# The first matmul of seven chunks as Strassen products, and the row sums of q as two columns of another matmul

## The chip, the cores and the metric

The kernel runs on one core of a Trainium2 chip. Such a core has five engines with instruction queues of their own: TensorE (PE in the profile; its weight loads are listed apart as PEld and overlap with its matmuls), VectorE (DVE), ScalarE (ACT), GpSimd (POOL) and SyncE (SP). Each works through its queue strictly in order, and an instruction that needs another engine's result waits at the head of its queue. SBUF is the on-chip memory that all engines use; PSUM is the small memory that TensorE writes its results to, here used as eight banks of 128 x 512 fp32 values. DMA transfers are issued on the queues of SP, POOL and ACT.

The metric is the time of one execution in device microseconds; smaller is better.

## The reference

Two layers follow each other. The first is a linear attention for 8 batches, 8 heads, 576 rows and a head size of 64; the second is a residual MLP behind a layer norm.

```python
q_s = exp(q) / sum over d;   k_s = exp(k) / sum over rows     # shifts left out
kv  = einsum('bhsd,bhse->bhde', k_s, v)
x   = einsum('bhsd,bhde->bhse', q_s, kv)  -> [8, 576, 512]     # heads side by side
xn  = (x - mean) / sqrt(var + 1e-6) * g_ln
out = x + relu(xn @ w_ch1) @ w_ch2                             # 512 -> 2048 -> 512
```

Inputs and output are fp32. The kernel multiplies in bf16 with fp32 sums.

## The kernel before

**Tiling.** A batch has 576 = 4 x 128 + 64 rows. Chunks `c` = 0 to 7 are the first 512 rows of one batch each, as `T` = 4 tiles of 128 rows; the ninth, `c = C9 = 8`, collects the last 64 rows of all eight batches, again 512 rows. Chunks are counted from 0 here, as in the code. Each chunk passes through attention, layer norm, a first matmul with `w1` (512 to 2048), ReLU, and a second with `w2` (2048 to 512).

**The two matmuls.** TensorE computes the hidden layer transposed: 16 row tiles `m` of 128 hidden units, each as four matmuls over `ko` (128 x 128 weights, up to 512 rows of the chunk as columns). `mm1` does a whole row tile, 512 columns wide; `mm1_part` does half, 256 columns, since the first row tiles start before all four `t` of the transposed input `xnT` have landed. In chunks 2 to 8 four row tiles run as halves and twelve whole. ScalarE applies the ReLU (L402 and L439) into `hT`. The second matmul is already in Strassen's form in chunks 1 to 8: `mm2_fast` runs seven products of 16 half-width matmuls (L521) into banks `a`, `b`, `c`, `e`; VectorE makes the sums of `hT` that they need (`sum_h`, L505), ScalarE and VectorE copy and add banks (L546, L619, L549), and VectorE finishes with a scale and the residual (L532), from where POOL's queue stores the result.

**Attention of the next chunk** runs beside the matmuls of the current one. k and v are loaded as fp32 on SP's queue (`load_batch`), q too; ScalarE takes `exp` of both and, from chunk 3 on, casts v to bf16 (`cast_v`, L157). `kv_mm` sums `exp(k)` times v on TensorE into a PSUM tile per two head pairs (`pkv`, one bank each; a column of ones in `vm` brings k's sums), and VectorE divides that into `kv_sb` as soon as the two head pairs of a tile are complete (`recip_z` at L243, two multiplications at L268). `eq_T` transposes `exp(q)` by DMA. `po_mm` then multiplies it with `kv_sb`, one bank `po` for each row tile. VectorE adds up q's rows beforehand (`reduce_q`, L199) and inverts the sums (L742); `x_fast` scales `po` with them into `x` (L338), takes the mean (L344), and writes `xn = (x - mean) * g` (L331). ScalarE sums the squares (L325), and a second DMA transpose (`xn_T`) makes `xnT` for the next chunk's first matmul.

**PSUM.** Pool `mm_ps` has six banks for everything about the two matmuls, pool `att_ps` has two tiles of one bank, which `pkv` and `po` share.

**Order.** The order in each queue is written out by hand. `mlp_steps(c)` lists TensorE's main steps with a weight each (1 for a matmul of 512 columns, 0.5 for 256), and `run` inserts the side work: a side function with position p is issued when the weights of the main steps before it have reached p. So a chunk of 64 + 56 = 120 units is the clock by which attention, sums, loads and transposes are placed. For chunks 2 to 6, `attn_fast` spreads `kv_mm` of the next chunk over positions 2 to 20 and the four groups of `po_mm` over 22 to 28, 36 to 43, 60 to 70 and 80 to 92.5; `second_side` does the like in chunk 1, `attn_rest` places the ninth chunk's attention into chunk 7.

Of the kernel before, what the change touches and what calls it, by code (L numbers as in the profile page):

```python
# [3 lines left out]

# [16 lines left out]
def kernel(  # L21
# [16 lines left out]
    nc = tc.nc  # L38
# [16 lines left out]
    CAST = (1, 2)  # L55
    T0 = 6
# [11 lines left out]
    att_ps = ctx.enter_context(tc.tile_pool(name="att_ps", bufs=2, space=PS))  # L68
    mm_ps = ctx.enter_context(tc.tile_pool(name="mm_ps", bufs=6, space=PS))

    ident = const.tile([P, P], BF16)
    eps_ln = const.tile([P, 1], FP32)
# [6 lines left out]
    g_bc = const.tile([P, DM], FP32)  # L79
# [3 lines left out]
    kv_sb = const.tile([P, B, NP, P], BF16)  # L83
# [18 lines left out]
    raws = {}  # L102

# [3 lines left out]
    def alloc_kv(b):  # L107
        raws[b][0], raws[b][1], raws[b][3], raws[b][4] = (
            raw.tile([P, H, T, D], FP32, tag="kt", name="kt", bufs=1),
            raw.tile([P, H, T, D], BF16 if b in CAST else FP32, tag="vt", name="vt", bufs=1),  # L110
# [50 lines left out]
    def prep_kvrem(b):  # L161
        par = b % 2
        nc.scalar.activation(ekr[:, par], raws[b][3], AF.Exp)
        for half in range(2):
            ps = slice(SR * half, SR * half + SR)
            nc.vector.tensor_copy(
# [4 lines left out]
    def new_eq(c):  # L171
        eqs[c] = (
            att.tile([P, T, H, D], BF16, tag="eq", name="eq"),
            sml.tile([P, T, H], FP32, tag="zq", name="zq"),
            sml.tile([P, T, H], FP32, tag="rq", name="rq"),
        )
        eqTs[c] = att.tile([P, T, NP, P], BF16, tag="eqT", name="eqT")
# [41 lines left out]
    def exp_k0(j):  # L219
        hs = slice(2 * j, 2 * j + 2)  # L220
        if j == 0:
            eks[0] = raw.tile([P, T0, H, D], BF16, tag="vt", name="ek0", bufs=1)
# [8 lines left out]
    def z0_mm(j):  # L231

        if j % 2 == 0:
            kvbox["z0", j // 2] = mm_ps.tile([P, 2, 256], FP32, tag="m", name="z0")
# [11 lines left out]
    def kv_mm(b, j, t):  # L246
        par = b % 2
        last = T if b else T0 - 1
        if j % 2 == 0 and t == 0:
            kvbox["p", j // 2] = att_ps.tile([P, 2, 256], FP32, tag="a", name="pkv")  # L250
# [12 lines left out]
        if j % 2 == 1 and t == last:  # L263
            js = slice(j - 1, j + 1)
            rzk = recip_z(pkv[:, :, P]) if b else kvbox["rz", j // 2]
            for half in range(2):
                ps = slice(64 * half, 64 * half + 64)
                nc.vector.tensor_mul(  # L268
                    kv_sb[ps, b, js, ps], pkv[ps, :, ps],
                    rzk[ps].to_broadcast([64, 2, D]),  # L270
                )

    def start_x(c):
# [3 lines left out]
            mlp.tile([P, T, DM], BF16, tag="xn", name="xn"),  # L277
# [6 lines left out]
    def po_mm(c, t, i):  # L284


        if c < B:
            if i == 0:
                pool, tag = (mm_ps, "m") if c == 0 and t >= 2 else (att_ps, "a")
                pobox["p"] = pobox[c, t] = pool.tile([P, DM], FP32, tag=tag, name="po")  # L290
            nc.tensor.matmul(  # L291
                pobox["p"][:, i * P : i * P + P], eqTs[c][:, t, i, :], kv_sb[:, c, i, :],
                start=True, stop=True,
            )
        else:
            if i % 2 == 0:
# [765 lines left out]
```

## Time and profile before

| | |
|---|---|
| median of 6 runs | 280.12 us (279.82 to 280.55) |
| the profiled execution's own time | 279.94 us |
| its span in the trace | 278.2 us (1.74 us lie around it) |
| PE busy | 272.0 us, 98% of the span, 2242 matmuls |
| DVE busy | 195.1 us, 70% |
| ACT busy | 181.8 us, 65% |
| granted TensorE clock | 0.999 of full speed |
| one chunk, c = 2 to 6 | 28.10 to 28.11 us from start to start |
| last chunk, c = 8 | 26.08 us |

How to read it: matmuls are pipelined, so a matmul of 256 columns is listed with 273 ns although the next one starts 109 ns later. For TensorE the distance between starts counts, and it is taken from a row of matmuls in the timeline. Times on VectorE and ScalarE are from start to end of one instruction; two that don't depend on each other may overlap by some 0.1 us.

### The profile page before, as it was taken

How to read it: one execution, taken by the hardware profiler on the slowest of the kernel's cores; microseconds unless marked ns; L12 is line 12 of the kernel's file. 1: busy time of each engine (PE TensorE's matmuls, PEld its weight loads, DVE VectorE, ACT ScalarE, POOL GpSimd, SP SyncE). 2: the span in 40 equal slices, each digit the busy share in tenths (PEclk: the TensorE clock that was granted, in tenths of full speed). 3: DMA queues.
4: the chain of work that ended last, by engine and by line, in shares of the span. 5: the costliest groups of instructions: out<-in, count | busy, mean ns of one | idle time of the engine just before them, and what ended most of it. 6: DMA issues, size and time to landing. Idle time of an engine off the chain costs nothing.

```text
span 278.2 us, 5663 instructions
## 1 busy us (share of the span) xinstructions
PE 272.0 (98%) x2242; PEld 201.5 (72%) x2245; DVE 195.1 (70%) x457; ACT 181.8 (65%) x346; POOL 36.8 (13%) x64
## 2 busy tenths in 40 slices
PE   8999999999999999999999999999999999999994
PEld 6788755766995699558955895599658855885683
DVE  4772648988996688658865886588657929962363
ACT  4578862797887785778577856786585477526500
POOL 3932124300030003000300030003000300030000
PEclk9999999999999999999999999999999999999999
DMA  7999999899969996994599469545914410241014
GB/s 197 247 206 209 336 215 334 196 251 320 170 168 370 281 129 174 326 219 79 146 338 230 81 161 303 107 75 133 209 39 78 138 52 1 40 128 61 2 38 113
DMA packets 68845, 48.01 MB, mean 173 GB/s; under 512 B 40402, under 2 KB 65490, under 8 KB 68819
## 3 DMA queue, kind: packets, MB, share of 16 engines
q1 hardware_dynamic: 57074, 27.66, 43.1%
q0 software_dynamic: 11152, 19.47, 27.9%
q10 hardware_dynamic: 592, 0.52, 0.6%
q8 instruction: 17, 0.28, 0.4%
q14 instruction: 10, 0.07, 0.1%
HBM read 36.70 MB, written 9.44 MB: 166 GB/s over the span
## 4 chain that ended last, share of the span: by engine, by line
PE 90%; DMA 5%; DVE 3%; POOL 1%; issue 0%; DVEq 0%
PE ph L414 29%; PE ba L521 20%; PE ph L429 15%; PE bb L521 5%; PE be L521 5%; PE bc L521 5%; PE pc L474 4%; DMA w_sb<-in_moe_w_ch_dram 3%; PE pkv L259 3%; PE po L291 2%; DMA qt<-in_q_dram 2%; DVE x L338 1%; DVE xn L331 1%; PE ptr L803 1%; PE po L298 1%; POOL v L866 1%
## 5 line engine op out<-in xcount | busy, mean ns | idle before, releaser
L414 PE MATMUL ph<-xnT,w_sb 128*128 128x512 bf16 x368 | 87.2, 379 | 0.0
L402 ACT ACTIVATE hT<-ph 128x512 bf16<-128x512 f32 x92 | 53.5, 598 | 18.4 <-PE ph L414 18.3
L414 PEld LDWEIGHTS <-w_sb 128*128 128x128 bf16 x368 | 34.1, 98 | 34.5 <-issue 0.2
L521 PEld LDWEIGHTS <-hs 128*128 128x128 bf16 x512 | 49.2, 98 | 5.8 <-DVE hs L505 0.2
L429 PE MATMUL ph<-xnT,w_sb 128*128 128x256 bf16 (+1 forms) x432 | 52.7, 269 | 0.3 <-DMA w_sb<-in_moe_w_ch_dram 0.3
L439 ACT ACTIVATE hT<-ph 128x512 bf16<-128x512 f32 x48 | 28.6, 599 | 24.5 <-PE ph L429 24.3
L505 DVE TENSOR_TENSOR hs<-hT 128x1024 bf16<-128x1024 bf16 x32 | 21.9, 687 | 27.8 <-ACT hT L402 27.6
L429 PEld LDWEIGHTS <-w_sb 128*128 128x128 bf16 x432 | 38.4, 98 | 4.2 <-DMA w_sb<-in_moe_w_ch_dram 0.5
L521 PEld LDWEIGHTS <-hT 128*128 128x128 bf16 x384 | 36.6, 98 | 5.2 <-ACT hT L402 0.2
L538 POOL DMA_DIRECT2D out_dram<-ot x28 | 15.0, 541 | 179.7 <-DVE ot L532 155.9
L521 PE MATMUL ba<-w_q,hs 128*128 128x256 bf16 x256 | 31.3, 273 | 0.0
L331 DVE SCALAR_TENSOR_TENSOR xn<-x,mv,g_bc 128x512 bf16<-128x512 bf16 x34 | 25.6, 752 | 1.2
L338 DVE SCALAR_TENSOR_TENSOR x<-po,rq 128x512 bf16<-128x512 f32 x30 | 20.6, 687 | 6.5 <-PE po L291 6.1
L325 ACT ACTIVATE scrap<-x,mv 128x512 bf16<-128x512 bf16 x34 | 24.6, 723 | 0.1
L291 PE MATMUL po<-kv_sb,eqT 128*128 128x128 bf16 x128 | 24.1, 219 | 0.4 <-DVE x L338 0.2
L199 DVE TENSOR_REDUCE zq<-eq 128x8 f32<-128x512 bf16 x32 | 20.1, 687 | 4.2 <-ACT eq L191 2.5
L259 PE MATMUL pkv<-vm,ek 128*128 128x129 bf16 x112 | 21.2, 220 | 0.0
L546 ACT COPY s<-ba 128x512 f32<-128x512 f32 x15 | 8.8, 584 | 16.7 <-PE ba L521 16.7
L291 PEld LDWEIGHTS <-eqT 128*128 128x128 bf16 x128 | 11.7, 98 | 7.4 <-issue 0.6
L521 PE MATMUL ba<-w_sb,hT 128*128 128x256 bf16 x128 | 16.2, 273 | 0.0
L521 PE MATMUL bb<-w_q,hs 128*128 128x256 bf16 x128 | 15.8, 273 | 0.0
L521 PE MATMUL bc<-w_sb,hT 128*128 128x256 bf16 x128 | 15.7, 273 | 0.0
(117 smaller groups left out, 337.9 us busy)
## 6 DMA issues: line engine op xcount, KB each, us to landing
out_dram<-ot POOLq DMA_DIRECT2D x32, 256.0 KB, 3.0
qt<-in_q_dram SPq DMA_DIRECT2D x5, 1024.0 KB, 7.4
kt<-in_k_dram SPq DMA_DIRECT2D x5, 1024.0 KB, 7.1
vt<-in_v_dram SPq DMA_DIRECT2D x5, 1024.0 KB, 10.8
w_sb<-in_moe_w_ch_dram POOLq DMA_DIRECT2D x8, 512.0 KB, 13.2
qt<-in_q_dram POOLq DMA_DIRECT2D x2, 1024.0 KB, 15.8
kt<-in_k_dram POOLq DMA_DIRECT2D x2, 1024.0 KB, 16.0
kt<-in_k_dram SPq DMA_DIRECT2D x4, 288.0 KB, 5.7
```

Source lines behind the costliest of these rows:

```text
L199: nc.vector.reduce_sum(eqs[c][1][:, t], eqs[c][0][:, t], axis=AX.X)
L259: nc.tensor.matmul(pkv[:, j % 2, 0:w], lhsT, rhs, start=(t == 0 and j % 2 == 0), stop=(t == last), skip_group_check=True,)
L291: nc.tensor.matmul(pobox["p"][:, i * P : i * P + P], eqTs[c][:, t, i, :], kv_sb[:, c, i, :], start=True, stop=True,)
L325: nc.scalar.activation(scrap, x[:, t], AF.Square, bias=mv[:, t, 0:1], accum_out=mv[:, t, 1:2])
L331: nc.vector.scalar_tensor_tensor(xn[:, t], in0=x[:, t], scalar=mv[:, t, 0:1], in1=g_bc, op0=ALU.add, op1=ALU.mult)
L338: nc.vector.scalar_tensor_tensor(x[:, t].rearrange("p (h d) -> p h d", h=H), in0=pobox[c, t].rearrange("p (h d) -> p h d", h=H), scalar=1. ...
L402: nc.scalar.activation(dst, src, AF.Relu)
L414: nc.tensor.matmul(hbox["ph"], w1_sb[:, ko, m * P : (m + 1) * P], xnTs[c][:, :, ko, :], start=(ko == 0), stop=(ko == KO1 - 1),)
L429: nc.tensor.matmul(ph[:, m % 2, at : at + tn], w1_sb[:, ko, m * P : (m + 1) * P], xnTs[c][:, t0 : t0 + tn, ko, :], start=(ko == 0), stop=( ...
L439: nc.scalar.activation(dst, ph, AF.Relu)
L505: nc.vector.tensor_tensor(out=dst, in0=x, in1=y, op=op)
L521: nc.tensor.matmul(hbox[bank][:, t], lhsT, rhs, start=first and (own or t == 0) and k == 0, stop=k == KH - 1, skip_group_check=True)
```

## The change

It touches four things.

1. **First matmul.** In chunks 2 to 8, row tiles 4 to 15 become three groups of four. Each group is a 2 x 2 block product (two row tiles of hidden units against two, two `ko` against two, columns of `t` 0, 1 against 2, 3) done as seven products of four matmuls 256 columns wide (`prod1`) in place of eight. The sums of weight blocks are made once, in chunk 1 (`quarter_w1`); the differences of `xnT` blocks once per chunk on VectorE (`sums_x`). Per group ScalarE copies a bank (`seed`) and keeps two intermediate sums in SBUF (`keep_g`), VectorE adds two banks (`seed_b`) and finishes one quarter with an addition and a ReLU (`last_g`). Row tiles 0 and 1 stay halves, 2 and 3 whole. `plan["order"]` (`o9` in the ninth chunk) is the sequence of these tokens.
2. **q's sums.** `kv_sb` gets two more columns per head pair, with ones, so that `po_mm` delivers 130 columns and the sums of `exp(q)` stand in two of them. VectorE inverts them in `x_fast`; `reduce_q` goes for chunks 1 to 7. A `po` tile is now two banks, and so is the one `pkv` tile of all four head pairs; pool `att_ps` holds a single such tile, which both use in turn. `kv_sb` is written when all of `kv_mm` is done.
3. **g.** The weight `g_ln` is multiplied into `w1` once (`fold_w1`, in chunk 0, behind its first matmul), and `x_fast` writes `512 * x - sum` with one input tensor in place of `(x - mean) * g` with two; the factor 512 goes out again in `rstd_op`.
4. **v.** From chunk 3 on, v is loaded by eight DMAs on POOL's queue, one per head, that cast to bf16 straight into `vm`. The casts on ScalarE go; the two small copies of `prep_kvrem` move from VectorE to ScalarE.

All positions of side work are set anew (`plan`); a chunk is 58 + 56 = 114 units. The core of the diff:

```diff
+    plan = dict(
+        order=('part 0|P1 0|C 0|part 2|x 0|P5 0|P6 0|x 1|P1 1|C 1|P2 0|E 0|P7 0|P6 1|L 0|P2 1|P3 0|P5 1|P4 0|P1 2|C 2|P7 1|E 1|plain 2|L 1|P6 2|P3 1|P4 1|P5 2|E 2|P7 2|P2 2|plain 3|P4 2|L 2|P3 2').split('|'),
+        kv=[12.5, 26.0],
+        po=[[29.0, 36.0], [45.0, 47], [55.0, 66.0], [85.0, 88.0]],
...
+        rest=[[20, 31, 36, 43.5], [38.0, 38.5, 58.0, 65.5], [51.5, 58.0, 65.0, 74.0], [63.5, 80.5, 85.0, 87.0]],
...
+        kv2=[42.5, 47.5],
+        po2=[[56.5, 56.5], [61, 63], [78.0, 81.0], [89.5, 92.5]],
...
-    att_ps = ctx.enter_context(tc.tile_pool(name="att_ps", bufs=2, space=PS))
+    att_ps = ctx.enter_context(tc.tile_pool(name="att_ps", bufs=1, space=PS))
...
-        if j % 2 == 0 and t == 0:
-            kvbox["p", j // 2] = att_ps.tile([P, 2, 256], FP32, tag="a", name="pkv")
...
+        if b and j == 0 and t == 0:
+            whole = att_ps.tile([P, NP, 256], FP32, tag="a", name="pkv")
+            for half in range(2):
+                kvbox["p", half] = whole[:, 2 * half : 2 * half + 2]
...
-        if j % 2 == 1 and t == last:
...
+        if t == last and (j == NP - 1 or b == 0 and j % 2 == 1):
+            for jj in ((j // 2,) if b == 0 else range(2)):
+                pkv = kvbox["p", jj]
+                js = slice(2 * jj, 2 * jj + 2)
+                rzk = recip_z(pkv[:, :, P]) if b else kvbox["rz", jj]
+                for half in range(2):
+                    ps = slice(64 * half, 64 * half + 64)
+                    nc.vector.tensor_mul(
+                        kv_sb[ps, b, js, ps], pkv[ps, :, ps],
+                        rzk[ps].to_broadcast([64, 2, D]),
+                    )
...
+        elif c < B:
+            if i == 0:
+                pobox[c, t] = att_ps.tile([P, NP, 256], FP32, tag="a", name="po")
+            nc.tensor.matmul(
+                pobox[c, t][:, i, 0:VW], eqTs[c][:, t, i, :], kv_sb[:, c, i, :],
+                start=True, stop=True,
+            )
...
+            po = pobox[c, t]
+            nc.vector.reciprocal(rq, po[:, :, P:VW])
...
+        if c:
+            nc.vector.tensor_scalar(
+                out=xs[c][2][:, t], in0=x[:, t], scalar1=float(DM), scalar2=st[:, t, 0:1],
+                op0=ALU.mult, op1=ALU.subtract,
+            )
+            return
...
+    def fold_w1(ko):
+        nc.vector.tensor_scalar_mul(
+            out=w1_sb[:, ko, :], in0=w1_sb[:, ko, :], scalar1=g_col[:, ko : ko + 1]
+        )
...
+            dst, x, y = ((t1, b12, b11), (t2, b22, t1), (t3, b22, b12), (t4, b21, t2))[n]
+            nc.vector.tensor_sub(out=dst, in0=x, in1=y)
...
+        nc.tensor.matmul(hbox["q", slot][:, m], lhsT, rhs, start=first and i == 0,
+                         stop=ko == 1, skip_group_check=True)
...
+        def seed(g, src, dst):
+            hbox["q", dst] = bank_of([P, 2, 2 * P], FP32, "q", dst)
+            nc.scalar.copy(hbox["q", dst], hbox["q", src])
...
+        def seed_b(g):
+            a_, b_, c_, e_ = names(g)
+            hbox["q", e_] = bank_of([P, 2, 2 * P], FP32, "q")
+            nc.vector.tensor_tensor(out=hbox["q", e_], in0=hbox["q", b_], in1=hbox["s2", g], op=ALU.add)
...
+            nc.vector.tensor_tensor(out=dst, in0=hbox["q", b_], in1=hbox["s3", g], op=ALU.add)
+            nc.vector.tensor_scalar_max(dst, in0=dst, scalar1=0.0)
...
+            nc.scalar.copy(hbox[name, g], hbox["q", 10 * g])
...
-            nc.vector.memset(raws[b][which][0:1, 0, 0, 0:1], 0.0)
+            if which != 1:
+                nc.vector.memset(raws[b][which][0:1, 0, 0, 0:1], 0.0)
...
+            for h in range(H):
+                nc.gpsimd.dma_start(
+                    vm[:, b % 2, :, h // 2, 64 * (h % 2) : 64 * (h % 2) + 64],
+                    v[b, h, 0:SM, :].rearrange("(p t) d -> p t d", t=T),
+                )
```

## The prediction

> **What bounds the kernel now.** I read the page from the top: who is busy, then what the chain that ended last is made of, then single chunks. TensorE leads, and the chain is matmuls nearly throughout:
>
> ```profile
> PE 272.0 (98%) x2242; PEld 201.5 (72%) x2245; DVE 195.1 (70%) x457; ACT 181.8 (65%) x346; POOL 36.8 (13%) x64
> ...
> PE 90%; DMA 5%; DVE 3%; POOL 1%; issue 0%; DVEq 0%
> PE ph L414 29%; PE ba L521 20%; PE ph L429 15%; PE bb L521 5%; PE be L521 5%; PE bc L521 5%; PE pc L474 4%; DMA w_sb<-in_moe_w_ch_dram 3%; PE pkv L259 3%; PE po L291 2%; DMA qt<-in_q_dram 2%; DVE x L338 1%; DVE xn L331 1%; PE ptr L803 1%; PE po L298 1%; POOL v L866 1%
> ```
>
> 98% busy could still hide stalls, since pipelined matmuls count as busy. So I compare a chunk's length with its matmuls. The chain in order of time has 48 matmuls of 512 columns in 10.36 us (0.2158 us each) and 16 of 256 columns in 1.746 us (0.1091); the timeline has kv's start 0.057 us apart and po's 0.0555. A chunk of 2 to 6 has 144 of 256 columns, 48 of 512, 20 for kv and 16 for po: 15.71 + 10.36 + 1.14 + 0.89 = 28.10 us. The table by stage shows as much from start to start:
>
> ```profile
> core 0: us, PE busy (x) PEld busy (x) DVE busy (x) ACT busy (x) POOL busy (x), PEclk, DMA share, GB/s
> 107.65:135.76 28.11, 28.11 (x230) 20.83 (x229) 20.82 (x50) 20.28 (x38) 1.75 (x4) 1.00 0.81 198
> 220.08:248.12 28.04, 28.04 (x210) 20.20 (x209) 21.19 (x42) 16.88 (x37) 2.21 (x5) 1.00 0.21 58
> 248.12:274.20 26.08, 26.08 (x192) 18.55 (x190) 11.71 (x23) 10.14 (x17) 1.21 (x3) 1.00 0.19 61
> ```
>
> TensorE doesn't wait at all in these chunks. Every matmul taken out is a gain in full, and every wait put in costs in full. VectorE and ScalarE are busy 74% and 72% of such a chunk.
>
> **Matmuls: the gain.** Per chunk, 48 of 512 and 32 of 256 columns become 8 of 512, 16 halves and 84 products of 256: 13.85 us becomes 1.73 + 1.75 + 9.16 = 12.64. That is 1.21 us, in seven chunks 8.5 us. A weight load takes 98 ns (group L521) and is hidden behind 109 ns; the second matmul has run at this pace all along. The two extra columns of po cost 112 x 0.001 = 0.1 us. Net -8.4 us, if nothing waits.
>
> **Average load of the others.** VectorE loses four reductions (0.687 each), a reciprocal (0.353), four means (0.153) and two casts (0.284), 4.3 us; four xn go from 0.752 to about 0.29, 1.9 us. It gains four differences of 512 bf16 elements, three `seed_b` of 0.70 (row L549), three `last_g` of 0.69 + 0.29 and four reciprocals of 0.20 (row L816): 7.5 us. So +1.4: 22.2 of 26.9 us. Three prices have no row. A difference lies between a copy of 512 (0.288) and the two-input row of 1024 (0.687); I take 0.42, above half the latter. The one-input bf16 operations (xn, the ReLU in `last_g`, `fold_w1`) lie between that copy and 0.752; I take 0.29, as the copy has the same types, size and memory:
>
> ```profile
> L331 DVE SCALAR_TENSOR_TENSOR xn<-x,mv,g_bc 128x512 bf16<-128x512 bf16 x34 | 25.6, 752 | 1.2
> L505 DVE TENSOR_TENSOR hs<-hT 128x1024 bf16<-128x1024 bf16 x32 | 21.9, 687 | 27.8 <-ACT hT L402 27.6
> L159 DVE COPY vm<-vt 128x512 bf16<-128x512 bf16 x8 | 1.8, 288 | 3.7 <-DMA vt<-in_v_dram 3.7
> ```
>
> ScalarE loses three ReLUs (0.60) and four casts (0.61), and gains nine copies of a bank (0.57 to 0.58) and two small copies (about 0.4): +1.8, 22.1 of 26.9. Both engines fit on average, so what counts is who waits in which order.
>
> **The new wait: kv to po.** Before, `pkv` has two tiles and the first half is divided while the second is still being summed; po comes after it at leisure. After, all four multiplications stand behind the last kv matmul, and po needs the same single tile of `att_ps`, so the first po waits until the fourth has read it. The trace has this very sequence once, in chunk 0, where kv's end comes in one piece:
>
> ```profile
> 43.21 0.13 PE pkv L259 x2
> 43.34 0.02 issue
> 43.36 0.18 DVE rzk L243
> 43.57 0.28 DVE kv_sb L268
> 43.86 0.29 DVE kv_sb L268
> 44.16 0.03 issue
> 44.19 0.18 DVE rzk L243
> 44.39 0.28 DVE kv_sb L268
> 44.69 0.30 DVE kv_sb L268
> 44.99 0.04 issue
> 45.03 0.29 PE po L291 x2
> ```
>
> By the timeline kv's last four start at 43.05 and every 0.057 us; the second closes the first half, so its slot on TensorE ends at 43.16 and its result is there at 43.34. From the end of the slot to po it takes 1.87 us with VectorE free. In the new order seven products stand between (the last of P3 0, P5 1, half of P4 0): 0.76 us. TensorE stands still for 1.10 us, in chunks 2 to 6, five times: +5.5 us. It can't be less while the chain is as it is. It can be more: VectorE's queue has `E 0` and `L 0` ahead of it. `L 0` waits for ScalarE's copy behind P7 0. I add up: P7 0 ends 4.99 us into the chunk, the copy at 5.77, the addition at 6.50, the ReLU at 6.83; kv's last slot ends at 6.70, and VectorE would start at 6.90. That leaves 0.07 us. All that makes one of these steps longer goes into the wait.
>
> **Other waits on TensorE.** In the same way I laid the three queues beside each other for one chunk. ScalarE's copies (`C`, `keep`) and `seed_b` end 0.1 to 0.6 us before TensorE needs them, so I charge nothing; 0.1 us too much in each of two places would cost 1 us over five chunks. The first differences end 2.0 us into the chunk, P6 0 starts at 2.6. In chunk 1, the second po at position 61 waits for `x_fast` of the first at 56.5: 0.20 + 0.20 + 0.77 + 0.09 = 1.26 us against 4.5 x 0.216 = 0.97: +0.3. Chunk 0 has this wait too, but loses the two of 0.2 us that it has now: 0. Chunk 7 has no kv, but ScalarE's pairs for the ninth chunk (L350 and L325, 0.63 + 0.20 + 0.72 + 0.20 = 1.74 us per row tile) in front of copies that TensorE now waits for, and four multiplications of 0.42 (L307) between one po and the next: I take 0.4 for po (four times 0.42 plus 0.25, 1.9 us, against 1.5 from position 56.4 to 63.5), 0.5 for P7 2 (12 products, 1.3 us, against one pair), and 0.3 for the copy of bank `c`: +1.2, bounds 0 and 2.
>
> **Work that is hidden.** `fold_w1` (four of 2048, about 0.7 each) and `quarter_w1` (four of 1536, about 1.0) lie in chunks 0 and 1, where VectorE has 2.7 us to spare in chunk 1 and more in chunk 0; without that cover up to 4 us would go into po. The extra small matmuls at the start stand before the wait of 0.3 us for w's load. On POOL, eight loads of v, 0.54 to 0.88 us each by rows L538 and L117, are 4.3 to 7 us; behind them only the stores at the end of the chunk are queued. They move 4096 pieces of 256 bytes where SP's load had 1024 of 1 KB. The queues' rows price a piece:
>
> ```profile
> q1 hardware_dynamic: 57074, 27.66, 43.1%
> q0 software_dynamic: 11152, 19.47, 27.9%
> ```
>
> 43.1% of 16 engines' 278.2 us over 57074 packets is 0.034 us each, for q0 it is 0.111: 4096 pieces on 16 engines take 8.6 to 28 us. I take 10, since q1's packets are the small ones, of 485 bytes on average. v is used a chunk after its issue, some 30 us; only in chunk 1 are there 22. On SP the k and q loads and transposes move up behind the missing v. The second `xn_T` lands some 2.2 us before it is needed, by its 3.1 us.
>
> [...]
>
> **Sum.** -8.4 + 5.5 + 0.3 + 1.2 = -1.4 us, on the profiled execution's 279.94 (span 278.2 plus 1.74). That execution is 0.18 us below the median; against 280.12 I say 278.7 us. The tail after the last matmul (3.9 us) stays.
>
> **Rivals.**
> *The full gain.* Chunks 2 to 6 don't wait for kv, for instance because TensorE is late there anyway. For it speaks only that no such wait is in the trace now; against it the chain above. 280.1 - 8.4 + 0.3 to 1.5: 272 to 273.5.
> *Slower: one-input operations at the price of xn.* If xn, the ReLU in `last_g` and `fold_w1` run at one element per step (0.69 for 512), each costs 0.40 more. The ReLU stands right before kv's division: +0.4 in five chunks. xn of the first row tile stands before `L 1`, which frees a bank for later products: another 0.4. That is 4 us, plus 0.5 for chunk 1, 0.5 for chunk 7, and in chunk 0 four `fold_w1` of 2.3 in place of 0.7, 6 us of VectorE of which 2 reach po: +7, hence 285.7. At 7 us for 0.40, the 1.4 are gone from 0.08 more: it decides from an operation of 0.37 us.
> *More small waits.* The margins of 0.1 us fail twice per chunk by 0.2: +2 us, 280.7.
> *v late.* At 28 us for the pieces v comes 6 us late in chunk 2, once: up to 284.7; halfway, 281.7.
>
> [...]
>
> **Chances.** Forecast 0.50 (277 to 280.2), full gain 0.13 (271.5 to 276), small waits 0.17 (279.7 to 282), VectorE's price 0.13 (282.5 to 287), v late 0.07 (280 to 285). 0.2% is 0.56 us, about what a measurement can tell. Faster: 0.45 + 0.13 = 0.58. Same: 0.05 of the forecast, 0.08 of the small waits, 0.01: 0.14. Slower: 0.28. The range 275 to 284 leaves out 0.08 on either side.
>
> **What would show it.** A wait of PE for kv_sb of 1.1 us in each of chunks 2 to 6, and none elsewhere above 0.5; chunks of 28.0 us instead of 28.1, a last one of 24.9; xn and the ReLU at 0.29. The forecast is wrong if chunks are at 27.0 (no wait), or above 28.4 with VectorE named.

## The result and the profile after

The changed kernel takes 281.44 us (median, 280.76 to 283.92) beside 280.24 us (279.82 to 280.94) for the kernel before, run on the same chip. The ratio is 1.0065 with a 95% interval of 1.0048 to 1.0082. It is slower by 1.2 us; the prediction said faster, 278.7 us. The profiled execution of the changed kernel took 281.55 us, with a span of 279.8 us, 1.6 us more than before.

The runs of the changed kernel fall into groups by the mean granted clock of TensorE, which each run records. Of the 17 runs on record, nine have a clock of 0.997 to 0.999 and lie at 280.76 to 281.32 us (median 280.95; below I call such runs, of any kernel, runs at full clock). The others: 0.989 at 281.55 (the profiled one), 0.991 at 282.8 to 282.95, and 0.983 at 283.67 to 283.92. The 80 runs of the kernel before that stood beside the experiments are all at 0.997 to 1.000. A mean of 0.995 need not be a low clock under work: in the changed kernel's profile 2.95 us at 0.50 lie behind the last matmul (276.81 us to the end of the span), where they cost nothing and alone take 0.005 off the mean, and the profile of e7 below has a mean of 0.995 with 1.00 in every window taken of it. This matters below, because the clock is one of the things that the prediction missed.

From the page of the changed kernel: the engines' busy time, the granted clock in 40 slices of the span, and what the chain that ended last is made of.

```profile
PE 266.9 (95%) x2446; PEld 221.9 (79%) x2449; DVE 210.7 (75%) x508; ACT 192.9 (69%) x379; POOL 68.4 (24%) x106
...
PEclk9979999999999999999999999999999999999997
...
PE 87%; DVE 7%; DMA 2%; issue 1%; ACT 1%; DVEq 0%
```

TensorE lost 5.1 us of work and the span grew by 1.6. VectorE's share of the chain has gone from 3% to 7%. The third slice, 14 to 21 us, is below full clock; so is the last one, but behind the last matmul.

What TensorE waited for in the whole run (engine, line waited for, total us, times, longest):

```profile
PE po L338 <- DVE kv_sb L306: 5.1, 5, 1.0
PE po L338 <- DVE x L398: 0.3, 2, 0.2
PE po L345 <- DVE x L355: 0.3, 1, 0.3
PE q L601 <- ACT s L673: 0.2, 1, 0.2
```

The wait for `kv_sb` is there five times, and nothing else in the chunks is above 0.3. The table by stage (chunk 3, chunk 7, and chunk 8 up to the start of its last VectorE instruction; chunk 8 begins with four matmuls of a product, at 249.34 us):

```profile
core 0: us, PE busy (x) PEld busy (x) DVE busy (x) ACT busy (x) POOL busy (x), PEclk, DMA share, GB/s
109.42:137.51 28.09, 27.07 (x259) 23.47 (x257) 22.11 (x56) 21.66 (x42) 8.09 (x13) 1.00 0.95 179
221.78:249.34 27.56, 27.08 (x238) 22.77 (x236) 25.28 (x55) 19.48 (x43) 2.20 (x5) 1.00 0.21 59
249.34:274.60 25.26, 25.18 (x222) 21.43 (x219) 17.36 (x36) 12.83 (x24) 1.51 (x4) 1.00 0.20 64
```

I take the start of each stage from the timelines of the two profiled executions and set the differences beside the prediction ("the last VectorE instruction" is its start, here and below; the end is good to 0.05 us, since the view gives the span to 0.1):

| stretch | before | after | difference | predicted |
|---|---|---|---|---|
| to the first matmul of chunk 0 | 17.08 | 18.52 | +1.44 | 0 |
| chunk 0 | 33.86 | 33.90 | +0.04 | 0 |
| chunk 1 | 28.44 | 28.91 | +0.47 | +0.3 |
| chunks 2 to 6 | 5 x 28.11 | 5 x 28.09 | -0.1 | -0.55 (-6.05 + 5.5) |
| chunks 7 and 8, to the last VectorE instruction | 54.32 | 52.78 | -1.54 | -1.2 |
| from there to the end of the span | 3.97 | 5.24 | +1.27 | 0 |

The sum is +1.58, the 1.6 us by which the span grew. The two stretches that I had costed at nothing, the start and the end, are the two large ones. The end, first before, then after the change:

```profile
274.23 0.48 DVE L561 SCALAR_TENSOR_TENSOR yl<-bd,rstd,yl 128x256 f32<-128x256 f32 x1 [0.39 <-PE bd L521]
```

```profile
274.46 0.54 POOL L796 DMA_DIRECT2D out_dram<-yl  x1 [23.07 <-DVE yl L786]
274.56 0.48 DVE L786 SCALAR_TENSOR_TENSOR yl<-bd,rstd,yl 128x256 f32<-128x256 f32 x1 [0.39 <-PE bd L745]
```

The start, in the chain in order of time. The second fence is the granted clock there (the number after the five engines' busy times):

```profile
10.00 1.05 PE gps L1125 x2
11.05 0.79 PE gcp L1129 x8
11.83 0.68 PE z L268 x24
12.52 1.36 PE pkv L295 x24
13.88 1.06 PE warm L926 x6
14.94 0.85 PE po L331 x8
15.80 2.15 PE warm L926 x12
...
18.52 0.27 PE ph L495 x2
```

```profile
12.00:14.00 2.00, 2.00 (x48) 1.98 (x46) 1.03 (x6) 0.00 (x0) 1.14 (x2) 1.00 1.07 267
14.00:16.00 2.00, 2.00 (x15) 1.65 (x14) 1.09 (x3) 0.80 (x2) 0.89 (x1) 0.50 1.23 206
16.00:18.00 2.00, 2.00 (x16) 1.57 (x14) 1.82 (x5) 1.04 (x3) 0.39 (x1) 0.65 1.25 208
```

The eight matmuls of `gcp` (one column each, for `g_col`) stand between `gps` and `z`, which are as thin. Some 1.6 us after this stretch of 2.5 us the clock drops to 0.50, and by the timeline the twelve warming matmuls take 2.36 us instead of 1.47. The same place before the change:

```profile
14.39 1.47 PE L695 MATMUL warm<-junk 128*128 128x256 bf16 x12
```

```profile
14.00:16.00 2.00, 2.00 (x23) 1.55 (x20) 1.57 (x5) 1.76 (x4) 0.89 (x1) 1.00 1.24 209
```

### The profile page after: what moved, and what is told of

Its sections match the earlier page's. It is cut to its first block, busy times and chain, and to the rows that moved or that the text cites. A ratio compares the mean times of both kernels' runs of the same rounds, so it can differ in the third digit from the quotient of the medians.

```text
span 279.8 us, 6311 instructions
## 1 busy us (share of the span) xinstructions
PE 266.9 (95%) x2446; PEld 221.9 (79%) x2449; DVE 210.7 (75%) x508; ACT 192.9 (69%) x379; POOL 68.4 (24%) x106
## 4 chain that ended last, share of the span: by engine, by line
PE 87%; DVE 7%; DMA 2%; issue 1%; ACT 1%; DVEq 0%
PE q L601 20%; PE ba L745 19%; PE ph L495 11%; PE ph L480 6%; PE bb L745 5%; PE bc L745 5%; PE be L745 5%; PE pc L540 5%; PE pkv L295 3%; PE po L338 3%; PE warm L926 2%; DVE kv_sb L306 2%; DMA qt<-in_q_dram 2%; PE ptr L1032 1%; DVE x L355 1%
## 5 line engine op out<-in xcount | busy, mean ns | idle before, releaser
L621 ACT ACTIVATE hT<-q 128x512 bf16<-128x512 f32 x63 | 36.7, 603 | 9.0 <-PE q L601 8.3
L601 PE MATMUL q<-ts,w_q 128*128 128x256 bf16 x252 | 38.2, 273 | 0.2 <-ACT s L673 0.2
L601 PEld LDWEIGHTS <-w_q 128*128 128x128 bf16 x336 | 31.4, 98 | 5.3 <-issue 0.5
L495 PEld LDWEIGHTS <-w_sb 128*128 128x128 bf16 x320 | 30.0, 98 | 3.7 <-issue 0.2
L1190 POOL DMA_DIRECT2D vm<-in_v_dram x40 | 29.7, 748 | 8.2 <-PE q L601 4.8
L505 ACT ACTIVATE hT<-ph 128x512 bf16<-128x512 f32 x34 | 20.3, 601 | 14.2 <-PE ph L495 14.0
L601 PEld LDWEIGHTS <-w_sb 128*128 128x128 bf16 x252 | 23.4, 98 | 3.9
L601 PE MATMUL q<-xnT,w_sb 128*128 128x256 bf16 x168 | 26.3, 273 | 0.0
L673 ACT COPY s<-q 128x512 f32<-128x512 f32 x42 | 24.5, 588 | 2.5 <-PE q L601 2.2
L338 PE MATMUL po<-kv_sb,eqT 128*128 128x130 bf16 x112 | 20.9, 220 | 5.5 <-DVE kv_sb L306 5.1
L480 PE MATMUL ph<-xnT,w_sb 128*128 128x512 bf16 x88 | 23.2, 379 | 0.0
## 6 DMA issues: line engine op xcount, KB each, us to landing
w_sb<-in_moe_w_ch_dram POOLq DMA_DIRECT2D x8, 512.0 KB, 14.2
```

The costliest lines, as they stand in the source:

```text
L338: nc.tensor.matmul(pobox[c, t][:, i, 0:VW], eqTs[c][:, t, i, :], kv_sb[:, c, i, :], start=True, stop=True,)
L480: nc.tensor.matmul(hbox["ph"], w1_sb[:, ko, m * P : (m + 1) * P], xnTs[c][:, :, ko, :], start=(ko == 0), stop=(ko == KO1 - 1),)
L495: nc.tensor.matmul(ph[:, m % 2, at : at + tn], w1_sb[:, ko, m * P : (m + 1) * P], xnTs[c][:, t0 : t0 + tn, ko, :], start=(m % 2 == 0 and a ...
L505: nc.scalar.activation(dst, ph, AF.Relu)
L601: nc.tensor.matmul(hbox["q", slot][:, m], lhsT, rhs, start=first and i == 0, stop=ko == 1, skip_group_check=True)
L621: nc.scalar.activation(hbox["h"][:, m0 : m0 + 2, 2 * nh : 2 * nh + 2], hbox["q", slot].rearrange("p m (t c) -> p m t c", t=2), AF.Relu,)
```

## The experiments

The theories, as the expectations name them. A: three separate costs, the wait from kv to po, gcp in the prologue, and a longer end. B: the clock falls wherever TensorE idles, in the chunks too. C: VectorE and ScalarE are at their limit, so a removed stall comes back elsewhere. F: the wait comes from the products' own load on VectorE. D: gcp, or the stretch of thin matmuls that it lengthens, lets the clock fall (D1 to D3 are forms of it); E: something else in the changed kernel does. G: two things lengthen the end, POOL's queue and a late first pair of stores.

### The wait from kv to po

**e3_po_later**

```diff
-        po=[[29.0, 36.0], [45.0, 47], [55.0, 66.0], [85.0, 88.0]],
+        po=[[34.5, 38.5], [45.0, 47], [55.0, 66.0], [85.0, 88.0]],
```

> Edit: the first po of chunks 3 to 7 moves from position 29 to 34.5, 1.19 us of matmuls later, nothing else. Theory A: the wait of PE for kv_sb goes (below 0.2 us), chunks 2 to 6 go from 28.09 to 26.9 to 27.2 us, the time falls by 4.5 to 6 us, to 275 to 277. Theory C (VectorE and ScalarE with 22 of 27 us used the stall to catch up): the wait comes back at x, s or hT elsewhere, chunks stay above 27.6 us, the time falls by less than 2.5 us. Theory B: full clock in every slice, as the stall is gone.

Measured: 278.04 us (277.11 to 279.34), ratio to before 0.9923 (0.9901 to 0.9944). The wait for `kv_sb` is gone from the list, and chunks 2 to 6 are 27.18 to 27.19 us each; chunk 3 in the table by stage:

```profile
108.62:135.81 27.19, 27.09 (x259) 23.45 (x257) 22.14 (x56) 21.62 (x42) 8.09 (x13) 1.00 1.01 185
```

The span of the profile is 275.3 us, 4.5 below the changed kernel's, and that is 5 x 0.90. Theory A holds for this term, though its 275 to 277 us are missed (the one run at full clock took 277.11), and C falls: of 1.19 us per chunk 0.29 came back, and by the starts in the timeline that is the second po, which now begins 0.27 us late; that it waits for `x_fast` of the first is read from the order of the code. B falls too. Its slices and runs still show a lower clock (0.984 to 0.993 in five of six runs) although the stalls are gone.

The chain in chunk 3 of the changed kernel shows the wait that was moved away:

```profile
116.06 0.06 PE pkv L295
116.11 0.11 PE q L601
116.22 0.07 PE pkv L295
...
117.63 0.30 DVE kv_sb L306
117.93 0.14 issue
118.07 0.22 PE po L338
```

The rows left out are VectorE's two `rzk` and three of the four `kv_sb`. From the end of kv's last slot (116.12) to po it is 1.95 us, of which seven products cover 0.76. TensorE stands still for 1.19 us.

**e7_plain**

```diff
     def mlp_steps(c):
-        if c >= 2:
+        if c == C9:
             return mm1_fast(c) + mm2_fast(c)
```

> Edit: chunks 2 to 7 with plain row tiles, as before the change; the last chunk keeps the products, and all chunks keep q's sums from TensorE and the single tile of att_ps. Chunks 2 to 6 then have 28.10 us of matmuls. Theory A (the products gain 1.21 us per chunk, the wait for kv_sb takes it back): with the wait still there 29.1 to 29.3 us per chunk, 281 + 6 x 1.2 = 287 to 289. Theory F (the wait comes from the products' own load on VectorE, E 0 and L 0 ahead of the divisions): without them the wait falls below 0.7 us, chunks at 28.3 to 28.8, 283 to 286.

Measured: 290.40 us (288.88 to 292.09), ratio 1.0353 (1.0318 to 1.0388), and in the table by stage for chunk 3

```profile
109.79:139.22 29.43, 28.29 (x231) 20.76 (x229) 15.88 (x43) 18.91 (x36) 8.10 (x13) 1.00 0.93 171
```

with `PE po L338 <- DVE kv_sb L306` at 1.1 us again (four times; the fifth, as long, is put down to a DMA of q). F falls: VectorE does 15.88 us in this chunk instead of 22.11, has no `E 0` and no `L 0`, and the wait is still there. It is longer: three plain matmuls (0.65 us) instead of seven products (0.76) cover the same chain, so 28.10 + 1.30. The products gain 29.43 - 28.09 = 1.34 us per chunk, the 1.21 of matmuls and 0.13 of better cover. Its three runs at 0.995 to 1.000 are at 288.9 to 289.5, at or slightly above what I expected: chunk 7 went from 27.56 to 29.44 us, 1.88 more in place of 1.2, with a wait of 1.1 us before a product of its second matmul.

### The start and the clock

**e1_gcol_dma**: `g_col` by a DMA.

```diff
-        gcp = bank_of([P, KO1], FP32, "gcp")
-        for ko in range(KO1):
...
-        nc.vector.tensor_copy(out=g_col, in_=gcp)
+        nbank[0] += 1
...
+                (20, lambda: nc.sync.dma_start(
+                    g_col, bass.AP(moe_g_ln.tensor, moe_g_ln.offset, [[1, P], [P, KO1]]))),
```

> Edit: g_col comes by a small DMA in chunk 0; the eight one-column matmuls of gcp leave the prologue. Theory A (three separate costs: the wait kv to po, the prologue's gcp, the end after the last store): the first matmul of chunk 0 starts at 17.0 to 17.3 us instead of 18.52, TensorE's clock stays at 1.00 between 14 and 18 us, the time falls by 0.6 us against undisturbed runs of the changed kernel and by 1.4 against its profiled execution: 279.9 to 280.3. Theory B (the clock falls because TensorE idles in any place, the 1.2 us stalls too): the prologue gains its 0.6 us, but the profile still shows slices below full clock. Theory C (the engines behind TensorE are at their limit): 0.6 us, as A.

Measured: 281.58 us (281.02 to 281.92), ratio 1.0038 (1.0026 to 1.0051). The clock is 0.995 to 1.000 in all five runs, as D would have it. The time is missed. The first matmul came at 18.15 us and now waits 0.4 us for w, and chunk 1's kv waits 0.5 for `vr`. By the order of the code SP has nothing ahead of this DMA of 512 values of 4 bytes, so I take it that it went out among the first loads; no view shows when. So the same was tried without a DMA.

**e5_gcol_vector**: `g_col` by VectorE in chunk 0.

```diff
+    def col_g(ko):
+        nc.vector.scalar_tensor_tensor(
+            g_dia, in0=gbox["g"][:, ko * P : ko * P + P], scalar=1.0, in1=ident,
+            op0=ALU.mult, op1=ALU.mult, accum_out=g_col[:, ko : ko + 1],
+        )
...
+                (26, lambda: [col_g(ko) for ko in range(KO1)]),
```

> Edit: the changed kernel without gcp; VectorE makes g_col in chunk 0 from the broadcast g and the identity, four instructions of 128 columns, about 0.25 us each, where it waits for v. No small DMA as in the first experiment. Theory D: no run below 0.995; 280.3 to 280.9, so about 0.3 us under the undisturbed runs of the changed kernel (280.95). If the small DMA of the first experiment cost nothing, 281.0 to 281.9 again, and then w's load, not gcp, sets the first matmul.

Measured: 280.89 us (280.33 to 281.80), ratio 1.0019 (1.0007 to 1.0032); clocks of 0.994 to 1.000 in twelve runs. The runs at 282.8 to 283.9 are gone. The run at 0.994 is the slowest (281.80), just below D's 0.995, and without a profile it stays open whether its clock fell under work. The 0.3 us expected from gcp's absence are not there: the median is that of the changed kernel at full clock (280.95), and in the profiles the first matmul comes 1.13 us earlier (17.39 us) but chunk 1 no earlier (52.55 against 52.42). So gcp's 0.8 us of TensorE were hidden, as the prediction said. What stands behind them is seen in TensorE's waits of this profile:

```profile
PE pkv L296 <- DVE vr L199: 0.5, 2, 0.3
PE pkv L296 <- DVE vm L192: 0.5, 1, 0.5
PE ph L496 <- DMA w_sb<-in_moe_w_ch_dram: 0.4, 1, 0.4
```

Chunk 0 waits at its end for batch 1's v to land and be copied: the copies `vm` start at 41.0 to 41.9 us in all sixteen profiles of this study, whenever chunk 0 started.

**b1_before_gcp**: the kernel before, with gcp added.

```diff
         nc.vector.tensor_copy(out=g_bc, in_=gps)
+        gcp = mm_ps.tile([P, KO1], FP32, tag="m", name="gcp")
+        for ko in range(KO1):
+            nc.tensor.matmul(
+                gcp[:, ko : ko + 1], g_row[:, ko * P : ko * P + P], ones_f[:, 0:1], start=True, stop=True
+            )
+        nc.vector.tensor_copy(out=g_col, in_=gcp)
```

> Edit: the kernel before, with the changed kernel's eight one-column matmuls (gcp) added to its prologue and nothing else. Theory D (these matmuls, between gps and z, are what lets the granted clock fall): a part of the runs at a clock of 0.983 to 0.993 and 0.6 to 3 us above 280.3, the others at 0.999 and 0 to 0.6 us above it. Rival E (the clock falls for another reason of the changed kernel, such as its stalls or its later loads): every run at 0.998 or above, and 280.3 to 280.9.

Measured: 280.75 us (280.26 to 283.62), ratio 1.0033 (1.0008 to 1.0058). Eight runs at 0.998 to 1.000 lie at 280.26 to 280.77, four at 0.988 to 0.992 lie at 282.54 to 283.62. That is D; E falls: of the 29 runs of the kernel before beside it, none is below 0.997. Eight matmuls of 0.8 us in all, put into the kernel before, make its clock fall in a third of the runs.

**e6_gcp_warm**: the changed kernel with `warm(6)` behind gcp.

```diff
         nc.vector.tensor_copy(out=g_col, in_=gcp)
+        warm(6)
```

> Edit: the changed kernel with six more warming matmuls of 256 columns (0.65 us) between gcp and z. Theory D, with the length of the unbroken stretch of small matmuls (gps, gcp, z: 2.5 us) as its cause: no run below 0.995, 281.3 to 281.9, that is 0.4 to 0.7 above the undisturbed runs. If the clock falls whatever stands between: a part of the runs at 0.983 to 0.993 as before, 282 to 285.

Measured: 281.62 us (281.08 to 283.36), ratio 1.0043 (1.0028 to 1.0058). Eleven runs at 0.996 to 0.999, one at 0.993 (283.36 us). The six matmuls protect the clock nearly always and cost what they take, 0.65 us. One run in twelve is against D's "no run below 0.995", and so against a strict rule by the length of the unbroken stretch.

**b2_gcp_early** and **b3_idle**: the kernel before, with gcp ahead of the twelve warming matmuls; and with idle time in place of gcp, by two exponentials on ScalarE whose result nobody uses.

```diff
             exp_k0(2 + t)
+            if t == 0:
+                gcp = mm_ps.tile([P, KO1], FP32, tag="m", name="gcp")
+                for ko in range(KO1):
...
+                nc.vector.tensor_copy(out=g_col, in_=gcp)
             warm((12, 5)[t])
```

```diff
             eq_pT(0, t, nc.scalar)
+            if t == 1:
+                for _ in range(2):
+                    nc.scalar.activation(
+                        scrap.rearrange("p (h d) -> p h d", h=H), q0[:, :, 0, :], AF.Exp
+                    )
             exp_k0(2 + t)
```

> Edit: the kernel before, with the same eight one-column matmuls, but ahead of the twelve warming matmuls instead of between gps and z. Theory D1 (it is the unbroken stretch gps, gcp, z that lets the clock fall): the stretch is back to the 1.8 us of the kernel before, so every run at 0.998 or above, 280.3 to 281. Theory D2 (the eight matmuls anywhere in the prologue are enough): a part of the runs at 0.983 to 0.993, 282.5 to 284, as where they stood between gps and z.

> Edit: the kernel before without any added matmul; two added exponentials on ScalarE (into scrap, unused) hold up the last piece of exp(k), so that TensorE stands idle about 0.8 us between gps and z. Theory D1, in the form that it is time without array work that counts: a part of the runs at 0.983 to 0.993, 1.5 to 3.5 us above the others. Theory D3 (one-column matmuls have a part of their own): every run at 0.998 or above, 280.3 to 281.5.

Measured for b2: 280.79 us (280.42 to 281.75), ratio 1.0023 (1.0012 to 1.0034), all twelve runs at 0.997 to 1.000, as the kernel before itself; five lie above the 281 us expected, up to 281.75, at full clock. For b3: 281.29 us (280.20 to 282.88), ratio 1.0038 (1.0015 to 1.0062); six runs at 0.998 to 1.000 (280.20 to 280.82), six at 0.992 to 0.994 (281.76 to 282.88). b3's timeline and clock:

```profile
10.04 1.12 PE L897 MATMUL gps<-g_row,ones_f 1*128 1x512 f32 x2
11.09 0.60 PE L236 MATMUL z<-ones,ek 96*128 96x1 bf16 x18
12.60 0.30 PE L236 MATMUL z<-ones,ek 96*128 96x1 bf16 x6 [0.90 <-ACT ek L223]
12.76 1.50 PE L259 MATMUL pkv<-v,ek 96*128 96x128 bf16 x24
```

```profile
12.00:14.00 2.00, 1.40 (x29) 1.41 (x30) 0.53 (x3) 0.54 (x1) 1.36 (x2) 1.00 1.07 261
14.00:16.00 2.00, 2.00 (x19) 1.68 (x17) 0.89 (x4) 0.63 (x1) 1.17 (x2) 0.56 1.24 210
16.00:18.00 2.00, 2.00 (x14) 1.54 (x13) 1.93 (x5) 1.21 (x3) 0.38 (x1) 0.59 1.25 206
```

D1 holds in the main, D2 and D3 fall. The same matmuls elsewhere do nothing to the clock, and idle time in their place does what they did. What tells the kernels apart is how long TensorE goes without full matmuls: 1.7 us in the kernel before (gps 10.21 to pkv 11.87) and no low clock, 2.5 us with gcp and a low clock in part of the runs, 2.7 us in b3 and a low clock in half of them.

Why it is only a part of the runs is not shown. The clock records in the traces of the two kernels hold this much: the granted clock changes only at whole multiples of 3.413 us after it first went full. In the changed kernel's it is full from 3.75 us, half from 13.99 (3 x 3.413 later), full from 17.40, and half again from 276.81 (80 x 3.413 after the first); in the kernel before's it is full from 4.56 us and half from 277.62 (80 x 3.413 later). So these points don't lie at the same place of the program in the two executions. In the four profiles with the fall (the changed kernel, e3, e8, b3; by the clock of their 2 us windows it begins at 13.99, 14.0, 13.8 and 14.2 us) the 3.4 us just before it hold all of gcp and z, or in b3 all of the idle time and z. That the place of these points against the thin stretch decides which runs fall is my guess: for the profiles without the fall no view shows the points, and no experiment moved them.

**b0_before**: the kernel before, unchanged, for a second profile.

> The kernel before, unchanged, for a second profile of it. If the 17.08 us to its first matmul of chunk 0 and the 50.94 us to chunk 1 are typical: within 0.3 us of these, and a clock of 1.00. If part of the 1.44 us that the changed kernel is late there is scatter in when the first loads land: 17.4 to 18.1 and 51.2 to 51.8.

Measured: 280.83 us; first matmul at 17.96 us, chunk 1 at 51.82, clock 1.000. So the second answer: of the 1.44 us between the two profiled executions up to 0.9 is scatter in when the first loads land. The chain of this profile shows it, since the same load of w1 sets the start in both profiles of before, from 7.97 us on in one and from 8.57 in the other:

```profile
8.57 9.34 DMA w_sb<-in_moe_w_ch_dram
17.96 0.28 PE ph L429 x2
```

### The end

**e2_last_store**

```diff
-        product(4, "a", ts=(0,), at={7: [lambda: stt(2, 0, hbox["a"][:, 0]), lambda: store(2, 1, 0, (nc.gpsimd, nc.sync))]})
+        product(4, "a", ts=(0,), at={7: [lambda: stt(2, 0, hbox["a"][:, 0]), lambda: store(2, 1, 0)]})
```

> Edit: the last but one pair of stores goes from SP's and ScalarE's queue again instead of POOL's and SP's. Theory A: from the last VectorE instruction to the end of the span 4.0 to 4.2 us as before the change, instead of 5.24; the time falls by 1.0 to 1.3 us. Rival: the end is set by the landing of the last bytes, whatever queue they are in; then the time changes by less than 0.3 us.

Measured: 282.53 us (279.94 to 283.39), ratio 1.0053 (1.0026 to 1.0080), with seven of twelve runs at 0.984 to 0.993. Its five runs at full clock have a median of 280.37, 0.6 below the changed kernel's 280.95. From the last VectorE instruction to the end it is 4.49 us instead of 5.24. So neither 4.0 to 4.2 us nor the rival's unchanged time came: POOL's queue costs about 0.7 us, and 0.5 remains.

**e8_last_order**: the last chunk's second matmul with the products and sums in the order of the kernel before.

```diff
-            15: [seed_c]})
-        product(5, "b", first=True)
-        product(6, "a", at={15: [lambda: copy_u("s2"), seed_e]})
-        product(2, "c", at={0: [lambda: both("b", 2, 1)], 15: [lambda: both("c", 0, 0), lambda: store(0, 2, 0)]})
-        product(7, "a", at={15: [
+            15: [lambda: both("a", 0, 0), lambda: sum_h(1, 2), lambda: sum_h(1, 3)]})
+        product(2, "c", first=True, at={15: [lambda: both("c", 0, 0, True), lambda: store(0, 2, 0)]})
+        product(6, "a", at={15: [lambda: copy_u("s2")]})
+        product(5, "b", first=True)
+        product(7, "a", at={1: [seed_e, lambda: both("b", 2, 1)], 15: [
...
-        product(4, "a", ts=(0,), at={7: [lambda: stt(2, 0, hbox["a"][:, 0]), lambda: store(2, 1, 0, (nc.gpsimd, nc.sync))]})
+        product(4, "a", ts=(0,), at={7: [lambda: stt(2, 0, hbox["a"][:, 0]), lambda: store(2, 1, 0)]})
```

> Edit: the changed kernel, but the last chunk's second matmul with the order of products, the sums on VectorE and the stores that the kernel before has. Theory G (two things lengthen the end: POOL's queue, 0.7 us, and the first pair of stores that is issued 3.6 us later, 0.5 us): from the last VectorE instruction to the end 3.9 to 4.1 us; the last chunk grows by 0 to 0.4 us, so the time is 280.0 to 280.6 in undisturbed runs, against 280.3 for the stores alone and 280.95 for the changed kernel. Rival: the end stays at 4.5 us, and the order of the products costs nothing there.

Measured: 282.73 us (280.91 to 284.13), ratio 1.0085 (1.0053 to 1.0116). The end is 4.35 us, so the order isn't what lengthens it, and G falls in its second half. The chunk is 26.47 us instead of 25.22, since TensorE now waits for VectorE:

```profile
PE ba L745 <- DVE yl L786: 1.1, 1, 1.1
```

The new order is thus worth 1.25 us. Without it the last chunk would be 0.19 us longer than in the kernel before (26.28), the products' 1.21 and more lost to that wait.

For the remaining 0.2 to 0.5 us of the end (4.20 to 4.49 in five profiles with these stores, 3.93 to 3.98 in five of the kernel before or its variants) there are only the two kernels' own traces, whose records of the queues' own instructions the views leave out; times are from the start of the last VectorE instruction. Behind the last stores SP waits for the semaphores of the DMA queues one after the other, in the same order in both (116, 101, 103, 104, 106, 107, 108, 117, 118), and one that is already met takes 0.06 us. In the kernel before the last bytes land at 2.94 us on the one but last of these (117), and SP is through at 3.09, 0.15 later. In the changed kernel they land at 3.34, on 103, so that six more follow: SP is through at 3.80, 0.46 later. That is 0.3 us from the order. Besides, a drain of POOL, which in the kernel before is over 20 us earlier, ends at 4.19, and one of VectorE ends 0.45 us after TensorE's (4.99 and 4.54; 3.45 and 3.48 before). Which of these remain in e2 and make its 0.5 us is not shown. No experiment changed the order of these waits.

The profile of e8 also caught a low clock at a worse place than the changed kernel's. kv of chunk 0 takes 2.40 us instead of 1.36, the first matmul comes at 19.92 us, and chunk 1 at 54.03 instead of 52.42.

### Together

**e4_all** (e1, e2 and e3), **e9_three** (e5, e2 and e3) and **e10_three_order** (e5, e3 and e8).

> The three edits together. Theory A: their sum, 281.4 - 0.6 - 1.2 - 5.5 = 273 to 275.5. Theory C: 277 to 278.5. Theory B: as A, with no run at a lower clock.

> Edit: g_col by VectorE in chunk 0, the first po 5.5 positions later, the last stores without POOL. Theories A, D and G together: no run at a clock below 0.995, no wait for kv_sb, 276.2 to 276.8, as with the small DMA in place of VectorE; 275.6 to 276.2 if that DMA had a cost of its own.

> As the one above, with the last chunk's order of products as before the change too. Theory G: the end 0.5 us shorter, the last chunk 0 to 0.4 us longer: the same time within 0.4 us, 275.8 to 276.8.

| kernel | us | ratio to before, 95% | lowest clock | chunks 2 to 6 | end |
|---|---|---|---|---|---|
| e4_all | 276.46 | 0.9861 (0.9848 to 0.9874) | 0.997 | 27.18 to 27.56 | 4.20 |
| e9_three | 275.93 | 0.9843 (0.9830 to 0.9856) | 0.997 | 27.18 to 27.20 | 4.32 |
| e10_three_order | 276.83 | 0.9882 (0.9868 to 0.9896) | 0.997 | 27.18 to 27.26 | 4.34 |

From the page of e9_three:

```profile
PE 265.7 (97%) x2438; PEld 219.9 (80%) x2441; DVE 211.3 (77%) x515; ACT 192.9 (70%) x379; POOL 66.8 (24%) x105
...
PEclk9999999999999999999999999999999999999999
```

e9_three beats both kernels, by 4.4 us the one before and by 5.5 the changed one. Against e5 it is 4.96 us faster: 5 x 0.90 from po and the rest from the store. Theory A's sum for e4 was too good by 1 to 3.5 us, as po gave 4.5 of the 5.5, gcp's 0.6 us were hidden and the end gave 0.7 to 1.0. e9 lies 0.5 us below e4, as expected if the small DMA has a cost of its own (four runs each, on two chips). e10 misses its "same time within 0.4 us": the old order in the last chunk costs 0.9 us there.

## Why the prediction was wrong, and where it was right

**Right: the gain of the products.** "in seven chunks 8.5 us": e7 gives 1.34 us per chunk, of which 1.21 are matmuls, and chunks 7 and 8 together gained 1.54 with their waits in (1.2 predicted).

**Right in mechanism, slightly short in size: the wait from kv to po.** 1.10 us were predicted in chunks 2 to 6 and 1.19 were there. The term mis-sized is the chain, 1.95 us instead of the 1.87 taken from chunk 0's row; the step from the last `kv_sb` to po alone is 0.14 us instead of 0.04. "VectorE's queue has `E 0` and `L 0` ahead of it" did no harm: in e7, without them, the chain is as long. Chunk 1's term was 0.47 instead of 0.3.

**Right: the prices.** From the groups of the changed kernel (busy time, mean ns):

```profile
L405 DVE TENSOR_SCALAR xn<-x,st 128x512 bf16<-128x512 bf16 x28 | 9.9, 354 | 1.1
L669 DVE TENSOR_SCALAR hT<-hT 128x512 bf16<-128x512 bf16 x21 | 6.3, 300 | 0.7
L584 DVE TENSOR_TENSOR ts<-xnT 128x512 bf16<-128x512 bf16 x14 | 5.8, 417 | 0.0
L1190 POOL DMA_DIRECT2D vm<-in_v_dram x40 | 29.7, 748 | 8.2 <-PE q L601 4.8 <-DMA out_dram<-ot 2.9 <-PE pkv L295 0.4
```

The ReLU at 0.30 us and xn at 0.35 (0.29 taken), the differences at 0.42 (0.42 taken); `fold_w1` took 0.82 (0.7 taken). The rival at xn's old price falls. The loads of v take 0.75 us of POOL each, within the 0.54 to 0.88 taken, and land after 8.5 us (median; 10 taken). In chunks 2 to 6 no matmul waits for them. The longest of the 40 issues keeps POOL 0.82 us.

**Wrong, first: the end.** The step that failed is "The tail after the last matmul (3.9 us) stays." It went from 3.97 to 5.24. The diff shows a store of the last chunk moved to POOL's queue, and that chunk's second matmul in another order; the four points of the change name neither, and I had only looked at what is queued behind POOL's loads of v. About 0.7 is that queue (e2). In the traces of the two kernels the order in which SP waits for the DMA queues at the end makes 0.3 us; how much of the 0.5 that e2 leaves is due to it is not shown.

**Wrong, second: the start.** The step that failed is "The extra small matmuls at the start stand before the wait of 0.3 us for w's load." On time it is right: e5 without them gains nothing at full clock, since w and v set the pace there. What it left out is that they stretch the thin work from 1.7 to 2.5 us and that TensorE's clock then falls in part of the runs. Of 59 runs of six kernels with that stretch (the changed one, e2, e3, e7, e8, b1) 30 are at 0.993 or below; of 29 runs of five kernels in which gcp was taken out (e1, e4, e5, e9, e10), none (one is at 0.994, as is one of the 59). It lifts the changed kernel's median from 280.95 to 281.44 and single runs by up to 3 us.

What is seen here is a clock of 0.50, in only part of the runs. In the four profiles that caught it, the rows around it add up to 3.4 us at 0.50 each time: for the changed kernel 2.0 us and 0.35 / 0.5 x 2.0 = 1.4 us. 2.5 us of thin work were enough, and they needn't be idle time: b3 has 0.9 us of idle time in its 2.7, in the other three profiles TensorE is busy throughout it.

**The sign.** Without these two steps the change comes out even: 280.95 at full clock less 0.6 to 0.7 for the store, or e2's 280.37 at full clock beside 280.31 for the kernel before. That is still not the 278.7 predicted. What is missing is read best from two profiles at full clock whose first matmul comes at nearly the same time, e2 (18.06 us, 280.73 us in all) and the second one of the kernel before (17.96 us, 280.83 us): -0.1 us instead of -1.4. By their starts of stages it is +0.6 in chunks 2 to 6 (+0.04 for -0.55, above all the longer chain), +0.5 to 0.6 at the end, +0.24 in chunk 0, +0.17 in chunk 1 (0.47 for 0.3), +0.1 at the start and -0.36 in chunks 7 and 8 (-1.56 for -1.2). Of the start's 1.44 us in the first table up to 0.9 is scatter of the loads (17.08 and 17.96 us in two profiles of before; 17.36 to 18.15 in seven of the changed kernel's variants at full clock without added warming).

None of the four rivals was the one that came. By size "v late" at halfway (281.7) is nearest to the median, and "more small waits" (280.7) to the runs at full clock, but no matmul of chunks 2 to 6 waited for v, and the small waits in the chunks were not there.

No profile fell into the runs at 0.983. An estimate from their clock speaks for a second stretch at half clock: 0.017 of 282 us is 4.8 us lost, a stretch of 3.4 us at 0.50 makes 1.7 of it, and the low clock behind the last matmul made 1.5 in the profiled execution. Where the second one lies is not shown.

## What to carry to other kernels

Read the start and the end of a trace with the same care as the steady chunks: here both were costed at nothing and together they took 2.7 us of the profiled execution (up to 0.9 of it scatter), nearly twice the predicted gain. A handful of one-column matmuls was cheap in time here and not in clock: eight of them, 0.8 us that e5 shows to be hidden, came with a low clock (0.993 or below) in 30 of 59 runs. Put them where full matmuls follow at once (b2: twelve runs, none below 0.997), or give the work to an engine that waits anyway (e5: twelve runs, none below 0.994). When a chain between two engines is longer than the work placed over it, try moving the consumer: 5.5 positions in the order gave 4.5 us here (shortening the chain was not tried).

## What the runs showed of the hardware

- TensorE's granted clock went to 0.50 for 3.4 us, 0.2 to 1.7 us after a stretch of 2.5 to 2.7 us with only one-row and one-column matmuls or idle time (four profiles: the changed kernel, e3, e8, b3); by the mean clock it fell in 30 of 59 runs with gcp behind gps, and after 1.7 us of the same in none of 80 runs of the kernel before. In the traces of the two kernels it changed only at whole multiples of 3.413 us after it first went full, at 4.56 us before and 3.75 us after the change. Five stalls of 1.2 us between full matmuls, 28 us apart, left it at full speed in the slices where they lie (changed kernel).
- With one of the last but one pair of stores (64 KB) in POOL's queue the end came 5.24 us after the start of the last VectorE instruction (changed kernel); with the pair in SP's and ScalarE's queues it came after 4.49 us (e2). POOL's store landed after 2.7 us, the others of the last chunk after 2.5 to 3.1; a drain of POOL ended at 4.19 us, 0.4 behind SP's last wait.
- The start of this kernel follows loads in POOL's queue (207 GB/s in all between 14 and 28 us): the first matmul that waits for w came at 17.08 and 17.96 us in two profiles of one kernel, the copies of v at 41.0 to 41.9 us in all sixteen profiles, and 0.8 us of TensorE's work ahead of them was hidden (e5).
- Each wait of SP for an already met semaphore at the end of the program took 0.06 us: where the semaphore of the last bytes was the third in order (changed kernel) SP was through 0.46 us after they had landed, and 0.15 us where it was the last but one (before).
